# A fused transform and ELU layer: contiguous row pairs, channel-128 sums moved one step later, and a tile's first products of the fourth accumulator put off

## The chip, the cores and the metric

The kernel runs on one core of one Trainium2 chip. The metric is the device time of one execution in microseconds. The engines are named as the profile names them: PE is TensorE with PEld for its weight loads, DVE is VectorE, ACT is ScalarE, POOL is GpSimd, SP is the sync engine, which here only issues DMAs. All executions in this document are of the state "fast". A "time" is that of the whole execution; a "span" runs from the first to the last instruction on the core and is about 2 us shorter.

## The reference

```python
X = np.fft.fft(x, axis=1); X = np.fft.fft(X, axis=2)      # x: 8 x 3008 x 256, float32
h = X.real.reshape(24064, 256) @ w_in                     # w_in: 256 x 2048
g = np.where(h > 0, h, np.exp(np.minimum(h, 0)) - 1)      # ELU
out = g @ w_out                                           # w_out: 2048 x 256
```

## The kernel before

The transform over the sequence uses its symmetries: rows are folded, and cosine and sine matrices turn the folded rows into two rings, Rr and Ir. The transform over the channels is folded into w_in, which becomes Wc and Ws. Channel 128 does not fit into 128 partitions and takes a path of its own. Its values are transformed with eight partitions, summed there (`ext_rows`), and broadcast into the ring Rb and row 127 of Ir.

The body is a list of 376 steps. Each makes two blocks of 128 hidden units for 256 columns:

```python
at(t + 0.0,  mm_P)         # TensorE: H  = Wc * Rr
at(t + 0.9,  even_part)    # VectorE: E  = Rb * wex + H
at(t + 2.17, mm_Q)         # TensorE: H += Ws * Ir          (after E has read H)
at(t + 3.55, h_minus)      # VectorE: second half of the outputs
... two activations each on ScalarE and VectorE (g_plus, g_minus), one step later
WINOGRAD = (sum_1, sum_3, sum_2, sum_4 on GpSimd,           # T + 2.91 to 2T + 0.3
            (2 * T + 0.87, mm_X1), (2 * T + 3.04, mm_X2))   # TensorE, seven products
```

`T` is 4.8, a nominal step; the times only fix the order on each engine. Eight steps make a tile of output columns in four PSUM accumulators, pA to pD. When a tile is full VectorE combines them, and the next tile reuses the same banks; this is called the turn of a tile below:

```python
def mm_X2(i):
    ...
    prod(i, 2, 0, wt(i, 2), 4)        # pC
    prod(i, 2, 1, wt(i, 0), 5)
    prod(i, 3, 0, wt(i, 3), 3)        # pD: in a tile's first step it waits for comb_3
    prod(i, 3, 1, w2b(i, 1, 1), 6)

COMB = ((1.45, comb_copy), (4.2, comb_1), (4.21, comb_2),
        (T + 1.0, comb_22),           # u: the last reader of pC
        (T + 2.5, comb_3))            # v: the last reader of pD
```

The parts that the change moves:

```python
# x rows behind s = 512: partition p holds rows 512 + 4(p % 64) + 2(p // 64) + 0, 1
for half in range(2):
    nc.sync.dma_start(out=L[j][64 * half : 64 * half + 64, 4 * ND :],
                      in_=xrows(b, row + 512 + 2 * half, 4, 64, 2))
...
at(33 * T + 1.46, lambda: ext_side(0)); at(33 * T + 1.47, lambda: ext_side(1))  # ScalarE copies
at(34 * T + 0.99, lambda: ext_rows(0, vtt))     # five sums on VectorE, even half
at(34 * T + 1.46, lambda: ext_side(2)); at(34 * T + 1.47, lambda: ext_side(3))
at(35 * T + 1.35, lambda: ext_rows(1, gtt))     # four sums on GpSimd, odd half
```

Of the kernel before, what the change touches and what calls it, by code (L numbers as in the profile page):

```python
# [18 lines left out]
ND = 256  # L19
# [15 lines left out]
def _dft_consts():  # L35







    p = np.arange(128)[:, None]
    out = np.zeros((128, 4, BW), np.float64)
    for ri in range(2):
        fn = np.cos if ri == 0 else np.sin
        for kodd in range(2):
            mat = out[:, 2 * ri + kodd]
            n, h = (NO, NO // 2) if kodd else (NE, NH)

            def block(m, n):
                k = 2 * np.arange(n)[None, :] + kodd
                s = 4 * p + m if m < 4 else 512 + 4 * (p % 64) + 2 * (p // 64) + m - 4
                w = np.where(s == 0, 0.5, 1.0) * (s <= RUN)
                w = np.where(s == RUN, 0.5 if ri == kodd else 0.0, w)
                return s, w * fn(2.0 * np.pi * ((s * k) % SEQ) / SEQ)

            for m in (0, 2, 4):
                s, v = block(m, h)
                anti = (s % 4 == 2) != ri  # L60
                if not kodd:
                    v[:, h - 1] *= ~anti[:, 0]
                if m < 4:
                    c = 0 if m == 2 * ri else h
                    mat[:, c : c + h] = v
                else:
                    mat[:, 2 * h : 3 * h] = v * ~anti
                    mat[:, 3 * h : 4 * h] = v * anti
            for t in range(3):
                mat[:, BE + t * NE : BE + t * NE + n] = block(2 * t + 1, n)[1]  # L70
    return out.reshape(128, -1).astype(np.float32)
# [36 lines left out]
def kernel(  # L108
# [43 lines left out]
    def row_tables():  # L152



        for c, p0, n, base in (
            (0, 0, 128, HALF - 3),
            (1, 0, 64, HALF - 513),
            (1, 64, 64, HALF - 515),
            (2, 0, 128, HALF - 3),  # L160
            (2, 0, 1, HALF - 4),
        ):
            pin(
                nc.gpsimd.iota(
                    ix[p0 : p0 + n, c : c + 1],
                    pattern=[[0, 1]],
                    base=base,
                    channel_multiplier=-4,
                )
            )  # L170

    def load_x(b):

        L = [
            spool.tile([128, 6 * ND], FP, tag=f"xl{j}", bufs=1, name=f"xl{j}")
            for j in range(4)
        ]

        def back(j, few):
            cols = slice(0, 2 * ND) if few else slice(2 * ND, 6 * ND)  # L180
            c = 1 if few else 2 if j == 1 and b == NB - 1 else 0
            pin(
                nc.gpsimd.indirect_dma_start(  # L183
                    out=L[j][:, cols],
                    out_offset=None,
                    in_=xflat,
                    in_offset=bass.IndirectOffsetOnAxis(
                        ap=ix[:, c : c + 1].bitcast(U32), axis=0
                    ),
                    element_offset=(b * SEQ + (HALF if j == 1 else 0)) * ND,  # L190
                )
            )
            if b == NB - 1 and j == 1 and not few:
                nc.gpsimd.dma_start(
                    out=L[1][0:1, 2 * ND : 5 * ND], in_=xrows(b, SEQ - 3, 1, 1, 3)
                )

        def ahead(j, row):
            nc.sync.dma_start(out=L[j][:, 0 : 4 * ND], in_=xrows(b, row, 4, 128, 4))
            for half in range(2):  # L200
                nc.sync.dma_start(
                    out=L[j][64 * half : 64 * half + 64, 4 * ND :],
                    in_=xrows(b, row + 512 + 2 * half, 4, 64, 2),
                )

        loads = [lambda n=n: back(2 - n // 2, n % 2) for n in range(4)]
        return L, loads + [lambda: ahead(3, HALF), lambda: ahead(0, 0)]


# [472 lines left out]
    def get_ext():  # L682
        xs = state["xs"] = spool.tile([128, 4, NB, 6], FP, tag="xs", bufs=1, name="xs")
        with nc.allow_non_contiguous_dma(reason="short runs"):
            for j in range(4):
                nc.sync.dma_start(
                    out=xs[:, j, :, 0:4],
                    in_=xe_dr[j, :, 0:512].rearrange("b (p m) -> p b m", m=4),
                )
                pairs = xe_dr[j, :, 512:768].rearrange("b (p h m) -> h p b m", h=2, m=2)  # L690
                for half in range(2):
                    nc.sync.dma_start(
                        out=xs[64 * half : 64 * half + 64, j, :, 4:6], in_=pairs[half]
                    )

    def fold_ext():
        xs = state["xs"]
# [29 lines left out]
    def ext_side(g, rows=NB):  # L727
# [3 lines left out]
        act(t[0:rows, 0:n], state["ext"][32 * g : 32 * g + rows, 0:n])  # L731
        state["side", par] = t

    def ext_rows(kodd, tt, rows=NB):
        n = NO if kodd else NE
        h = (n + 1) // 2
        if not kodd or rows < NB:
            rx = spool.tile([128, HALF + 1], FP, tag="rx", bufs=1, name="rx")
            state["rx"] = rx[0:rows]
        rx, even, b = state["rx"], state["side", 0], state["side", 1][0:rows]  # L740
        a = spool.tile([128, NE], FP, tag="bs", bufs=3, name="bs")
        unfold(a, even, even[:, h : 2 * h], rows, n, tt)
        a = a[0:rows]
        o, base = 1 - kodd, kodd * RUN
        m = n - 2 * o
        tt(rx[:, base : base + n], a[:, 0:n], b[:, 0:n], ALU.add)
        top = base + RUN - 1
        tt(rx[:, top : top - m : -1], a[:, o : o + m], b[:, o : o + m], ALU.subtract)
        if not kodd:
            tt(rx[:, HALF:], a[:, 0:1], b[:, 0:1], ALU.subtract)  # L750
            nc.sync.dma_start(
                out=r4_dr.rearrange("o b -> b o"), in_=rx[:, HALF : HALF + 1]
            )
        nc.sync.dma_start(
            out=r128_dr[0:rows, base : base + RUN], in_=rx[:, base : base + RUN]
        )
# [140 lines left out]
    def wt(i, j):  # L897
        return WT[j][:, i % 8]
# [31 lines left out]
    def mm_X2(i):  # L930
        T = tiles[i // 8]
        if i % 8 == 0:
            T.acc += [bank(t) for t in ACC[2:4]]
        prod(i, 2, 0, wt(i, 2), 4)
        prod(i, 2, 1, wt(i, 0), 5)
        prod(i, 3, 0, wt(i, 3), 3)
        prod(i, 3, 1, w2b(i, 1, 1), 6)
        del steps[i]
# [300 lines left out]
    for slot in range(total):  # L1239
        i = slot % 2 * 8 + slot // 2 if slot < 16 else slot  # L1240
        t = slot * T
        begin = (
            (0.0, mm_P),
            (0.4 if slot == 0 else 0.9, even_part),
            (2.17, mm_Q),
            (3.55, h_minus),
            (4.2, below_plus),
            (4.8, below_minus),
            (T + 0.01 if slot < 16 else T + 1.5, exp_plus),
            (T + 0.02 if slot < 16 else T + 2.21, exp_minus),  # L1250
        )
        if slot == 1:
            begin = (
                (0.1 - T, mm_P),
                (0.7 - T, even_part),
                (2.6 - T, mm_Q),
                (1.5, h_minus),
                (2.95, below_plus),
                (3.0, below_minus),
                (3.01, exp_plus),  # L1260
                (3.02, exp_minus),
            )
        for dt, fn in begin + (
            (T + 2.2, g_plus),
            (T + 2.9, g_minus),
        ) + (
            (
                (2 * T + 0.87, lambda i: mm_plain(i, 0)),
                (2 * T + 3.04, lambda i: mm_plain(i, 1)),
            )  # L1270
            if i < 16
            else WINOGRAD
        ):
            at(t + dt, lambda fn=fn, i=i: fn(i))
    COMB = (
# [77 lines left out]
    at(9 * T + 4.75, dft_ext_0)  # L1353
    for g in (2, 3):
        at(10 * T + 1.46, lambda g=g: ext_side(g, 1))
    at(11 * T + 3.55, lambda: ext_rows(1, gtt, 1))
    at(11 * T + 3.6, lambda: spread_ext(0, 1))
    for n in range(16):
# [7 lines left out]
    at(32 * T + 4.75, dft_ext)  # L1366
    at(33 * T + 1.46, lambda: ext_side(0))
    at(33 * T + 1.47, lambda: ext_side(1))
    at(34 * T + 0.99, lambda: ext_rows(0, vtt))
    at(34 * T + 1.46, lambda: ext_side(2))  # L1370
    at(34 * T + 1.47, lambda: ext_side(3))
    at(35 * T + 1.35, lambda: ext_rows(1, gtt))
    fold_keys = [(k, p) for k in FOLDS for p in range(2 if k[0] not in "cx" else 1)]
    n_big = sum(k[0] not in "cx" for k, _ in fold_keys)
    for b in range(1, NB):
# [26 lines left out]
                lambda k=2 * ri + kodd: state["EO"][k],  # L1402
            )
        for kodd in range(2):
            step = s0 + (35 if late else 28, 38 + late)[kodd]
            assert step >= safe(b * HALF + (kodd + 1) * RUN)
            at(step * T + 1.0, lambda b=b, kodd=kodd: spread_ext(b, kodd))
    last = total - 40
# [49 lines left out]
```

## Time and profile before

| quantity | before |
|---|---|
| time, median of the first three runs | 1960.54 us (1960.31 to 1960.62) |
| span of the profiled run | 1958.7 us |
| PE busy | 99% of the span |
| DVE, ACT, POOL busy | 66%, 44%, 70% |
| undisturbed step | 4.75 us |
| step 34 | 9.32 us |
| granted clock in steps 34 and 35 | 0.87 and 0.90; 0.50 (the half clock below) from 227.5 to 230.9 us |

A kernel whose TensorE is busy for 99% of the span can gain only in the gaps. These are read from the waits of PE and from the lengths of the steps, each counted from one step's first Wc product to the next. A busy share hides them.

### The profile page before, as it was taken

The page shows a single profiled execution, that of the slowest core. Times are in us where ns is not written, and L with a number is a line of the kernel's source. Part 1 is how long each engine was busy: PE and PEld are TensorE (multiplying, and loading weights), DVE is VectorE, ACT ScalarE, POOL GpSimd, SP SyncE. Part 2 cuts the span into 40 slices and gives each one's busy share as a digit, 9 for nine tenths or more (in the row PEclk, how much of TensorE's full clock was granted, in tenths as well). Part 3 has the DMA queues.
Part 4 walks back from the last instruction along what each step waited for, and adds up shares of the span by engine and source line. Part 5 has one row for each costly group of instructions (what it writes and reads, how often), then busy time and mean ns, then how long its engine had stood idle before and what let it go on. Part 6 is the DMA issues. An engine that isn't in the chain of part 4 may idle for free.

```text
span 1958.7 us, 27031 instructions
## 1 busy us (share of the span) xinstructions
PE 1938.8 (99%) x8912; PEld 1652.8 (84%) x8912; DVE 1296.1 (66%) x2393; ACT 864.8 (44%) x1669; POOL 1379.6 (70%) x1821
## 2 busy tenths in 40 slices
PE   8999999999999999999999999999999999999998
PEld 5788788888888888888888888888888888888887
DVE  8976566666667666666666665676666766666666
ACT  3654344444444444444344444444434444344443
POOL 3888767776687766777677876778667776555655
PEclk9999999999999999999999999999999999999999
DMA  8246120111111021010210202002020110100101
GB/s 309 66 30 45 36 52 20 33 29 24 44 20 44 14 43 30 18 46 14 53 24 12 49 10 59 12 19 59 6 53 11 20 22 15 17 12 12 23 10 24
DMA packets 263611, 70.26 MB, mean 36 GB/s; under 512 B 248926, under 2 KB 249842, under 8 KB 263472
## 3 DMA queue, kind: packets, MB, share of 16 engines
q1 hardware_dynamic: 257680, 55.69, 15.2%
q0 software_dynamic: 3616, 12.59, 2.1%
q8 instruction: 70, 1.15, 0.2%
q14 instruction: 69, 0.57, 0.1%
q10 hardware_dynamic: 2176, 0.26, 0.1%
HBM read 43.66 MB, written 24.80 MB: 35 GB/s over the span
## 4 chain that ended last, share of the span: by engine, by line
PE 92%; POOL 2%; DVE 2%; DMA 2%; issue 1%; ACT 1%; SPq 0%; DVEq 0%; POOLq 0%; ACTq 0%
PE H L414 37%; PE pD L414 16%; PE pC L414 16%; PE pB L414 16%; PE pA L414 8%; DMA xl<-in_x_dram,ix 1%; DMA raw<-in_moe_w_out_dram 1%; POOL WT L423 1%; POOL w L423 1%; POOL G L423 0%; DMA raw<-in_moe_w_in_dram 0%; DVE E L810 0%; POOL xl L183 0%; DVE G L836 0%; DVE v L420 0%
## 5 line engine op out<-in xcount | busy, mean ns | idle before, releaser
L423 POOL TENSOR_TENSOR G<-G 128x256 f32<-128x256 f32 x1440 | 1034.6, 728 | 515.9 <-DVE G L836 343.2
L810 DVE SCALAR_TENSOR_TENSOR E<-Rb,wex,H 128x256 f32<-128x256 f32 x752 | 328.1, 478 | 582.1 <-PE H L414 578.4
L426 ACT ACTIVATE G<-H 128x512 f32<-128x512 f32 x376 | 224.5, 597 | 960.2 <-DVE G L820 960.2
L414 PE MATMUL H<-Ir,Ws 128*128 128x256 f32 x1504 | 386.9, 380 | 2.5 <-DVE E L810 1.3
L414 PE MATMUL H<-Rr,Wc 128*128 128x256 f32 x1504 | 387.7, 380 | 0.0
L414 PE MATMUL pC<-G,WT 128*128 128x256 f32 x1440 | 369.6, 379 | 1.6 <-DVE u L420 1.6
L414 PEld LDWEIGHTS H<-Rr,Wc 128*128 128x128 f32 x1504 | 285.1, 190 | 56.6 <-issue 3.4
L414 PEld LDWEIGHTS H<-Ir,Ws 128*128 128x128 f32 x1504 | 277.2, 189 | 51.9 <-DVE E L810 3.9
L414 PEld LDWEIGHTS pC<-G,WT 128*128 128x128 f32 x1440 | 273.5, 190 | 39.1 <-issue 2.0
L820 DVE SCALAR_TENSOR_TENSOR G<-E,H 128x512 f32<-128x512 f32 x376 | 257.1, 684 | 35.1 <-PE H L414 1.6
L836 DVE SCALAR_TENSOR_TENSOR G<-G,H 128x512 f32<-128x512 f32 x376 | 255.9, 681 | 21.6 <-ACT G L426 21.5
L836 DVE SCALAR_TENSOR_TENSOR G<-M,G 128x512 f32<-128x512 f32 x376 | 257.1, 684 | 0.0
L426 ACT ACTIVATE G<-G 128x512 f32<-128x512 f32 x376 | 233.2, 620 | 0.0
L414 PE MATMUL pD<-G,w 128*128 128x256 f32 x784 | 229.8, 380 | 0.7 <-POOL G L423 0.7
L414 PE MATMUL pA<-G,w 128*128 128x256 f32 x784 | 229.3, 379 | 0.6 <-DVE bs L420 0.6
L414 PE MATMUL pB<-G,w 128*128 128x256 f32 x784 | 229.3, 379 | 0.0
L426 ACT ACTIVATE M<-G 128x512 f32<-128x512 f32 x376 | 224.3, 596 | 0.0
L426 ACT ACTIVATE M<-M 128x512 f32<-128x512 f32 x376 | 221.0, 588 | 0.0
L414 PE MATMUL pD<-G,WT 128*128 128x256 f32 x720 | 215.3, 381 | 2.9 <-DVE v L420 2.5
L414 PE MATMUL pB<-G,WT 128*128 128x256 f32 x720 | 214.5, 379 | 0.2
L414 PEld LDWEIGHTS pD<-G,w 128*128 128x128 f32 x784 | 149.2, 190 | 21.4 <-POOL G L423 1.1
L414 PEld LDWEIGHTS pA<-G,w 128*128 128x128 f32 x784 | 148.9, 190 | 21.1 <-issue 0.9
(145 smaller groups left out, 1418.2 us busy)
## 6 DMA issues: line engine op xcount, KB each, us to landing
out_dram<-ot SPq DMA_DIRECT2D x496, 32.0 KB
xl<-in_x_dram SPq DMA_DIRECT2D x16, 512.0 KB
xl<-in_x_dram SPq DMA_DIRECT2D x32, 128.0 KB
out_dram<-ot SPq DMA_DIRECT2D x256, 2.0 KB
Rb<-r SPq DMA_DIRECT2D x10, 376.0 KB
raw<-in_moe_w_in_dram SPq DMA_DIRECT2D x7, 512.0 KB
MC<-dft_mats SPq DMA_DIRECT2D x3, 943.5 KB
raw<-in_moe_w_out_dram SPq DMA_DIRECT2D x4, 512.0 KB
```

Of the source, the lines that this page charges most:

```text
L414: nc.tensor.matmul(out_, lhsT=lhsT, rhs=rhs, start=start, stop=stop, skip_group_check=True)
L423: pin(nc.gpsimd.tensor_tensor(out=o, in0=a, in1=b, op=op))
L426: pin(nc.scalar.activation(out=o, in_=i, func=func, **kw))
L810: nc.vector.scalar_tensor_tensor(out=S.E[:, c], in0=Rb[:, cols(i)], scalar=wex[:, f : f + 1], in1=S.H[:, c], op0=ALU.mult, op1=ALU.add,)
L820: nc.vector.scalar_tensor_tensor(out=two(S.G[:, 0:512])[:, :, ::-1], in0=two(S.E), scalar=2.0, in1=two(S.H), op0=ALU.mult, op1=ALU.subtract,)
L836: nc.vector.scalar_tensor_tensor(out=o, in0=e, scalar=-1.0, in1=h, op0=ALU.add, op1=ALU.max)
```

## The change

Its intent has three parts. Two contiguous rows per partition behind s = 512 make one DMA of two. The channel-128 sums of the even half leave step 34, which also turns a tile over, for VectorE's gap in step 35; those of the odd half leave GpSimd in step 35 for VectorE's gap in step 36. And in a tile's first step the products into pD come after the next step's Wc products, so that they need not wait for v.

```diff
-   s = 4 * p + m if m < 4 else 512 + 4 * (p % 64) + 2 * (p // 64) + m - 4
+   s = 4 * p + m if m < 4 else 508 + 2 * p + m
    (the row tables and the loads of channel 128 follow; one iota and one DMA of each pair go)
-   for half in range(2):
-       nc.sync.dma_start(out=L[j][64 * half : 64 * half + 64, 4 * ND :],
-                         in_=xrows(b, row + 512 + 2 * half, 4, 64, 2))
+   nc.sync.dma_start(out=L[j][:, 4 * ND :], in_=xrows(b, row + 512, 2, 128, 2))
    ...
+   def ext_unfold(kodd, tt, rows=NB): ...        # the first two sums of ext_rows, cut off
    ...
+   def mm_X3(i):
        prod(i, 3, 0, wt(i, 3), 3)
        prod(i, 3, 1, w2b(i, 1, 1), 6)
    ...
+   X3 = ((3 * T + 0.1 if i % 8 == 0 else 2 * T + 3.05, mm_X3),)
    ...
-   at(34 * T + 0.99, lambda: ext_rows(0, vtt))
-   at(34 * T + 1.46, lambda: ext_side(2))
-   at(34 * T + 1.47, lambda: ext_side(3))
-   at(35 * T + 1.35, lambda: ext_rows(1, gtt))
+   at(35 * T + 0.2, lambda: ext_unfold(0, vtt))
+   at(35 * T + 1.5, lambda: ext_rows(0, vtt))
+   at(35 * T + 4.75, lambda: ext_side(2))
+   at(35 * T + 4.76, lambda: ext_side(3))
+   at(36 * T + 0.2, lambda: ext_unfold(1, vtt))
+   at(36 * T + 1.5, lambda: ext_rows(1, vtt))
    (the broadcast of the even half goes from step 35 to step 37)
```

More of the change, by code (lines that the diff above doesn't have):

```diff
@@ L152, in row_tables @@
     def row_tables():
-        for c, p0, n, base in (
-            (0, 0, 128, HALF - 3),
-            (1, 0, 64, HALF - 513),
-            (1, 64, 64, HALF - 515),
-            (2, 0, 128, HALF - 3),
-            (2, 0, 1, HALF - 4),
+        for c, n, base, step in (
+            (0, 128, HALF - 3, -4),
+            (1, 128, HALF - 513, -2),
+            (2, 128, HALF - 3, -4),
+            (2, 1, HALF - 4, 0),
         ):
@@ L164, in row_tables @@
                 nc.gpsimd.iota(
-                    ix[p0 : p0 + n, c : c + 1],
+                    ix[0:n, c : c + 1],
                     pattern=[[0, 1]],
                     base=base,
-                    channel_multiplier=-4,
+                    channel_multiplier=step,
                 )
@@ L199, in ahead @@
             nc.sync.dma_start(out=L[j][:, 0 : 4 * ND], in_=xrows(b, row, 4, 128, 4))
-            for half in range(2):
-                nc.sync.dma_start(
-                    out=L[j][64 * half : 64 * half + 64, 4 * ND :],
-                    in_=xrows(b, row + 512 + 2 * half, 4, 64, 2),
-                )
+            nc.sync.dma_start(
+                out=L[j][:, 4 * ND :], in_=xrows(b, row + 512, 2, 128, 2)
+            )
         loads = [lambda n=n: back(2 - n // 2, n % 2) for n in range(4)]
@@ L689, in get_ext @@
                 )
-                pairs = xe_dr[j, :, 512:768].rearrange("b (p h m) -> h p b m", h=2, m=2)
-                for half in range(2):
-                    nc.sync.dma_start(
-                        out=xs[64 * half : 64 * half + 64, j, :, 4:6], in_=pairs[half]
-                    )
+                nc.sync.dma_start(
+                    out=xs[:, j, :, 4:6],
+                    in_=xe_dr[j, :, 512:768].rearrange("b (p m) -> p b m", m=2),
+                )
     def fold_ext():
@@ L732, in ext_side, with ext_unfold @@
         state["side", par] = t
+    def ext_unfold(kodd, tt, rows=NB):
+        n = NO if kodd else NE
+        h = (n + 1) // 2
+        even = state["side", 0]
+        a = spool.tile([128, NE], FP, tag="bs", bufs=3, name="bs")
+        unfold(a, even, even[:, h : 2 * h], rows, n, tt)
+        state["es"] = a[0:rows]
     def ext_rows(kodd, tt, rows=NB):
         n = NO if kodd else NE
-        h = (n + 1) // 2
         if not kodd or rows < NB:
@@ L739, in ext_rows @@
             state["rx"] = rx[0:rows]
-        rx, even, b = state["rx"], state["side", 0], state["side", 1][0:rows]
-        a = spool.tile([128, NE], FP, tag="bs", bufs=3, name="bs")
-        unfold(a, even, even[:, h : 2 * h], rows, n, tt)
-        a = a[0:rows]
+        rx, a, b = state["rx"], state["es"], state["side", 1][0:rows]
         o, base = 1 - kodd, kodd * RUN
@@ L1271 @@
             if i < 16
-            else WINOGRAD
+            else WINOGRAD + X3
         ):
@@ L1355 @@
         at(10 * T + 1.46, lambda g=g: ext_side(g, 1))
+    at(11 * T + 3.54, lambda: ext_unfold(1, gtt, 1))
     at(11 * T + 3.55, lambda: ext_rows(1, gtt, 1))
@@ L1404 @@
         for kodd in range(2):
-            step = s0 + (35 if late else 28, 38 + late)[kodd]
+            step = s0 + (37 if late else 28, 38 + late)[kodd]
             assert step >= safe(b * HALF + (kodd + 1) * RUN)
```

## The prediction

> **What bounds the kernel now.** I read the page first, then TensorE's own waits, then a table of stretches cut at the starts of the steps, then the order of instructions inside the stretches that stood out. The page gives TensorE 1938.8 of 1958.7 us, and its chain of the work that ended last is 92% TensorE.
>
> ```profile
> PE 1938.8 (99%) x8912; PEld 1652.8 (84%) x8912; DVE 1296.1 (66%) x2393; ACT 864.8 (44%) x1669; POOL 1379.6 (70%) x1821
> ...
> PE 92%; POOL 2%; DVE 2%; DMA 2%; issue 1%; ACT 1%; SPq 0%; DVEq 0%; POOLq 0%; ACTq 0%
> ```
>
> The change removes no matmul: as many products, transforms and transposes run as before. An undisturbed step starts 22 TensorE records and takes 4.75 us (241.57 to 246.32). The change can win only where TensorE stands still or runs at a lower clock. Its waits, longest first (total us, times, longest):
>
> ```profile
> PE pC L414 <- DVE xe L420: 3.1, 1, 3.1
> PE pD L414 <- DVE v L420: 2.5, 4, 1.0
> PE pC L414 <- DVE u L420: 1.6, 1, 1.6
> PE H L414 <- DVE E L810: 1.3, 3, 0.6
> ```
>
> The first falls at 15 us in the start-up. The second and third are the change's aim: pC and pD are the third and fourth accumulator, whose first product of a new tile waits until VectorE has combined the old tile (u reads pC, v reads pD). The table of stretches, one step each (columns: length, busy time of PE, PEld, DVE, ACT, POOL, then granted clock, DMA):
>
> ```profile
> 220.58:229.90 9.32, 6.42 (x24) 4.46 (x23) 7.59 (x15) 3.91 (x8) 5.15 (x8) 0.87 0.16 40
> 229.90:235.16 5.26, 5.26 (x23) 4.54 (x22) 3.38 (x6) 2.10 (x5) 5.10 (x8) 0.90 0.03 7
> 235.16:241.57 6.41, 6.29 (x29) 5.12 (x28) 3.38 (x6) 2.47 (x5) 6.10 (x9) 1.00 0.33 51
> 241.57:246.32 4.75, 4.75 (x23) 4.15 (x22) 3.19 (x7) 1.79 (x4) 2.70 (x5) 1.00 0.54 104
> ```
>
> Step 34 takes 9.32 instead of 4.75 us, steps 35 and 36 lose some more, and the clock is down in the first two. Step 36 holds half a transform beside its products (1.28 us by its matmuls), so only 6.41 - 4.75 - 1.28 = 0.4 of it is waiting. Inside step 34:
>
> ```profile
> 223.09 1.30 DVE L420 TENSOR_TENSOR bs<-side 8x189 f32<-8x189 f32 x2
> ...
> 224.43 1.07 DVE L420 TENSOR_TENSOR rx<-bs,side 8x377 f32<-8x377 f32 x3
> ...
> 225.43 0.40 DVE L420 TENSOR_TENSOR u<-v,pC 128x256 f32<-128x256 f32 x1
> ...
> 225.59 0.48 ACT L426 ACTIVATE side<-H 8x376 f32<-8x376 f32 x1 [0.63 <-DVE rx L420]
> ...
> 225.97 1.10 PE L414 MATMUL pC<-G,WT 128*128 128x256 f32 x4 [1.61 <-DVE u L420]
> ...
> 227.23 0.68 DVE L420 TENSOR_TENSOR v<-v,pD 128x512 f32<-128x512 f32 x1
> ...
> 228.06 1.19 PE L414 MATMUL pD<-G,WT 128*128 128x256 f32 x2 [0.98 <-DVE v L420]
> ```
>
> Five channel-128 sums (2.34 us of VectorE) stand ahead of u, in the one step that also has to turn a tile over. They hold u, u holds pC; ScalarE waits for them with its next copies and passes the delay to the activation, to v and to pD.
>
> [...] The lower clock costs 9.32 x 0.13 + 5.26 x 0.10 = 1.7 us. [...] the first bs took 1039 ns beside a GpSimd fold that ended at 223.92, the second, of the same size and alone, 335. [...] this run shows only the cost of issuing, 1.19 us for two of them.
>
> **The change part by part.**
>
> Row pairs. Each batch's load issues two DMAs fewer on the sync engine, of about 0.6 us each, and the start-up one row-table instruction of 0.13 us fewer on GpSimd. Bytes and packet sizes stay (2 KB rows). In the first 16 us the DMA engines run at 300 to 400 GB/s nearly throughout, so an earlier issue only lengthens the backlog, and VectorE's first fold waits for the landing at 10.74 us. I put 0 on it, and 0.7 either way.
>
> Fourth accumulator. A list of the tile turns shows v late for pD at eight of them: step 34 and seven others. Counting start to start against the usual 216 ns and the slow refill behind each wait, four of the seven (472, 517, 913 and 1441 us) lose 0.32 us and three (956, 1001, 1398 us) lose 0.78, 0.71 and 0.78: 3.55 us. The rest lose nothing; there v ends 0.42 us before pD starts. Put off behind the next step's first four records, these products start 0.86 us later, more than the wait. But what then comes sooner has limits of its own. At 956 us the step's next product group would reach its third pair, which needs GpSimd's third sum, at 955.93 + 3 x 0.86 = 958.52, and that sum ends at 957.17 + 2 x 0.75 = 958.67 or so: with the refill, about 0.35 us of the 0.78 comes back. At the short turns the sum is in time (474.1 against 474.4). So 4 x 0.32 + 3 x 0.42 = 2.5 us.
>
> Channel-128 sums. I walk step 34 to 36 by the measured spacings (0.61 us for an activation pass on VectorE, 0.78 for the pair of E, 0.86 for four TensorE records). Step 34: u at 223.09, in time for pC at 224.2; the activation pass, v, and the other passes run through to 225.9. TensorE begins step 35 at 225.06. Step 35 on VectorE: unfold 225.9 to 227.1 (two operations of 0.34 alone, a GpSimd sum in the way of each), E to 228.0, in time for TensorE, which wants it by 228.08; three sums to about 229.3; two passes, h and a transpose to 231.8. VectorE is full by then. Step 36 begins on TensorE at 230.67. ScalarE copies the odd half only after step 35's h, at 231.75 to 232.7, so the second unfold starts at 232.25 and ends[...] between 233.3 and 233.9; E(36) ends near 234.4. TensorE wants it at 232.83. So I expect one new wait of 1.4 to 2.0 us before the Ws products of step 36. Then 234.45 + 3 x 0.86 + 1.28 + 0.1 of refill: step 37 at 238.4 instead of 241.57, a gain of 3.1 us, v's late pD of step 34 and the old clock loss in it. A new wait of 1.6 us in one piece may bring the half clock back. [...] I give it 4 in 10, so 0.4 x 1.7 = 0.7 off: 2.4 us.
>
> Moving the odd sums from GpSimd frees it of 3.0 us in step 35 and with it the 0.4 us of waiting for GpSimd's sums in step 36; that is in the walk. The broadcast of the new row to Rb now goes out after the stores of tile 3, near 242 us; it is first read in step 40, near 254, so it is hidden.
>
> Sum: 2.4 + 2.5 + 0 = 4.9, and 1960.5 - 4.9 = 1955.6; I take 1955.4, since the walk places contention on every operation.
>
> **Rivals.** (a) The new wait at step 36 does not occur, because VectorE finds GpSimd idle at the right moments or ScalarE copies sooner. For it: before the change VectorE stood idle 2.38 and 1.22 us ahead of E in steps 35 and 36, which is what the change wants to fill. Against it: with 2.3 us more in each of two steps that have 2.6 us of passes and a 0.6 us transpose, VectorE needs about 5.5 of the 5.6 us that step 35 then lasts[...]. It would make 1952.7. (b) VectorE becomes the bound for the two steps and the half clock returns: gain near step 34 about 1 us, and 1957.5. (c) The products put off collide with what follows, so that the seven turns move their wait on to GpSimd's sums or to a bank of H: then only the four short ones gain, 1.3 us, and the whole gives 1956.7. (d) Start-up: earlier issued matrices delay the x rows that VectorE waits for; 0.5 to 1 us worse.
>
> **Range and chances.** Everything in play is TensorE waiting of 5.5 us around steps 34 to 36 and 3.55 us at seven turns; all of it together would give 1951.4 without start-up effects. (a) bounds the likely side below at about 1952, (b) with (d) above at about 1958.3. A change of 2% is 39 us, four times all of it, so the answer is "within 2%" almost surely.
>
> **What would show it.** Right, if step 34 shrinks to about 4.5 us with no wait for u; if no turn shows TensorE waiting for v; if the odd unfold runs on VectorE in step 36 beside a wait of TensorE for E of over a microsecond; and if the three long turns show a short wait for GpSimd's sums. Wrong, if steps 35 to 36 show no wait (then faster than I say), if a second half-clock window of 3.4 us stands near 235 us (slower), if the first product on TensorE starts more than 0.7 us off its 28.54, or if a turn that lost nothing before waits now.

## The result and the profile after

The changed kernel took 1953.19 us in the median (1952.0 to 1954.94, four runs) against 1960.58 (1960.31 to 1960.75, four runs). The ratio is 0.9963, 95% interval 0.9946 to 0.998. A ratio here is the mean time of one kernel's fast runs over that of the other's of the same rounds, so it is not quite the ratio of the medians quoted. By the 2% rule this is "same". The profiled run was the slowest of the four.

From the page of the changed kernel, busy times and the shares of the chain that ended last:

```profile
PE 1936.6 (99%) x8912; PEld 1653.8 (85%) x8912; DVE 1299.7 (67%) x2397; ACT 865.1 (44%) x1669; POOL 1378.4 (71%) x1816
...
PE 93%; DVE 3%; POOL 2%; issue 1%; DMA 1%; ACT 1%; SPq 0%; DVEq 0%; POOLq 0%
```

As many matmuls as before, and still 99%: the page alone would not say that anything happened. The four extra DVE instructions and four of the five fewer on POOL are the odd sums that changed engine. PE's own waits (total us, times, longest) do say it:

```profile
PE pC L410 <- DVE xe L416: 3.2, 1, 3.2
PE H L410 <- DVE E L809: 2.6, 4, 1.2
...
PE pD L410 <- POOL G L419: 0.7, 1, 0.7
```

The waits of pD for v (2.5 us) and of pC for u (1.6 us) are gone. The waits for E rose from 1.3 to 2.6 us in all, 1.2 of it in one piece. The steps 34 to 37 of the changed kernel (length, then busy times, clock, DMA share, GB/s):

```profile
220.90:225.38 4.48, 4.17 (x20) 3.23 (x19) 4.38 (x9) 2.12 (x4) 3.92 (x6) 1.00 0.00 0
225.38:230.99 5.61, 5.61 (x28) 4.87 (x27) 5.61 (x11) 2.12 (x4) 3.47 (x5) 1.00 0.02 4
230.99:238.84 7.85, 6.56 (x30) 5.04 (x29) 6.63 (x13) 4.26 (x8) 5.93 (x9) 1.00 0.24 38
238.84:243.59 4.75, 4.75 (x24) 4.16 (x23) 3.19 (x7) 1.81 (x4) 3.11 (x5) 1.00 0.39 70
```

Step 34 is only 4.48 us long because its pD products (0.86 us) now run in step 35, which is that much longer; 0.59 us of it is still a wait for E with its refill (the product behind the first one started 0.32 us after it, where 0.22 is usual; the step takes 3.89 us in odd38_side below). The clock stays at 1.00. Steps 34 to 36 together take 17.94 us instead of 20.99: 3.05 us less. In step 35 DVE (third busy figure) works for all 5.61 us. The price is in step 36: 7.85 us, of which 4.75 are a step's own work and 1.28 half a transform. The order of instructions shows where the rest goes:

```profile
223.41 0.41 DVE L416 TENSOR_TENSOR u<-v,pC 128x256 f32<-128x256 f32 x1
...
224.51 1.03 PE L410 MATMUL pC<-G,WT 128*128 128x256 f32 x4
...
226.13 1.31 DVE L416 TENSOR_TENSOR bs<-side 8x189 f32<-8x189 f32 x2
...
228.15 1.77 DVE L416 TENSOR_TENSOR rx<-bs,side 8x377 f32<-8x377 f32 x3
...
232.38 0.98 ACT L422 ACTIVATE side<-H 8x376 f32<-8x376 f32 x2
...
232.88 1.14 DVE L416 TENSOR_TENSOR bs<-side 8x188 f32<-8x188 f32 x2 [0.55 <-ACT side L422]
...
233.95 0.85 DVE L809 SCALAR_TENSOR_TENSOR E<-Rb,wex,H 128x256 f32<-128x256 f32 x2
...
234.86 1.13 PE L410 MATMUL H<-Ir,Ws 128*128 128x256 f32 x4 [1.22 <-DVE E L809]
```

The number in brackets is the engine's idle time before the instruction. In step 34, u is done well before pC asks for it. In step 36 the odd sums wait for ScalarE's copy, E waits for the odd sums, and PE waits 1.22 us for E.

At the seven other tile turns no wait for v is left. The three long ones keep a shorter one of another kind; the turn at 952 us of the changed kernel:

```profile
953.45 2.34 POOL L419 TENSOR_TENSOR G<-G 128x256 f32<-128x256 f32 x3 [0.40 <-DVE G L835]
...
955.04 0.70 PE L410 MATMUL pB<-G,WT 128*128 128x256 f32 x2
```

The pB products would have started at 954.81 after the pair before them. They need the second of the three sums in the POOL line, and the step loses 0.34 us where it lost 0.78.

### The profile page after: what moved, and what is told of

It is laid out like the page before. It is cut to its first block, busy times and chain, and to the rows that moved or that the text cites. A ratio compares the mean times of both kernels' runs of the same rounds, so it can differ in the third digit from the quotient of the medians.

```text
span 1953.2 us, 26991 instructions
## 1 busy us (share of the span) xinstructions
PE 1936.6 (99%) x8912; PEld 1653.8 (85%) x8912; DVE 1299.7 (67%) x2397; ACT 865.1 (44%) x1669; POOL 1378.4 (71%) x1816
## 4 chain that ended last, share of the span: by engine, by line
PE 93%; DVE 3%; POOL 2%; issue 1%; DMA 1%; ACT 1%; SPq 0%; DVEq 0%; POOLq 0%
PE H L410 37%; PE pC L410 16%; PE pD L410 16%; PE pB L410 16%; PE pA L410 8%; POOL WT L419 1%; POOL w L419 1%; POOL G L419 0%; DMA xl<-in_x_dram 0%; DVE E L809 0%; DVE e L504 0%; DVE G L835 0%; DVE o L504 0%; DVE pow L310 0%; DMA xl<-in_x_dram,ix 0%
```

## The experiments

Eleven runs were made, nine of new kernels and two repeats, all with correct results. Differences of one or two microseconds are not safe in the medians, because the start-up turned out to move by that much (see below). So I read every kernel twice: by its time, and by its steps in one profile. "Start" is the first Wc product of step 0, "0 to 37" the time from there to that of step 37, "37 to 372" the time from there to that of step 372. One difference in the column "0 to 37" belongs to no edit: step 4 took 6.91 to 6.93 us in eight profiles, with one wait of PE for GpSimd's weight work of 0.6 us, and 6.36 or 6.37 us without it in five (same_again, dft_late, halves_back, sel_dft, sel_dft_x).

| kernel | median us | ratio to before | start | 0 to 37 | 37 to 372 |
|---|---|---|---|---|---|
| before | 1960.58 | | 28.54 | 213.03 | 1685.01 |
| changed | 1953.19 | 0.9963 | 28.86 | 209.98 | 1682.47 |
| rows_only | 1960.54 | 0.9994 | 28.71 | 213.14 | 1684.89 |
| x3_only | 1959.35 | 0.9994 | 28.86 | 213.07 | 1682.66 |
| ext_only | 1959.09 | 0.9991 | 29.47 | 209.97 | 1684.91 |
| whole_again | 1953.88 | 0.9966 | 26.42 | 210.00 | 1682.27 |
| same_again | 1961.81 | 1.0003 | 29.61 | 212.51 | 1685.07 |
| x_first | 1953.81 | 0.9965 | 25.86 | 210.06 | 1682.52 |
| odd38_side | 1951.58 | 0.9952 | 28.32 | 207.90 | 1682.49 |
| dft_late | 1956.12 | 0.9974 | 28.56 | 209.47 | 1684.51 |
| halves_back | 1955.41 | 0.9975 | 30.20 | 209.40 | 1682.42 |
| sel_dft | 1950.05 | 0.9949 | 26.82 | 207.28 | 1681.61 |
| sel_dft_x | 1948.16 | 0.9939 | 26.19 | 207.29 | 1681.21 |

**rows_only.** The kernel before with the first part of the diff alone.

```diff
+   s = ... 508 + 2 * p + m       # with its row tables, loads and channel-128 loads, nothing else
```

> The kernel before with the row pairs alone (new order of rows behind 512, one DMA in place of two, one row-table instruction fewer). Theory A (the start-up is free of it on average, as predicted): 0 against before, within 0.7 us, and as steady as before (spread under 0.5 us). Theory B (the 2.2 us by which the whole change beat my number come from here, and so does the spread of 1952.0 to 1954.9 that the kernel before does not have): 1 to 3 us faster in the median, with single runs spread over 1.5 us or more, and the first product of step 0 between 25.5 and 29 us instead of 28.54, moved by the landing of the first x rows.

The runs fell into two groups: 1958.15 and 1958.70, and 1960.54 to 1961.08. The spans do the same: twice 1956.3, and 1958.2, 1958.4, 1958.6, while the nine runs of the kernel before beside them had 1958.2 to 1959.2. So theory B holds in part: the spans are spread, two of five are some 2.3 us shorter, and in their mean the edit is worth 1958.68 - 1957.56 = 1.1 us, with five runs. Its gain of 1 to 3 us in the median did not come (1960.54 against 1960.63), and the profiled run is one of the longer ones. The DMA view of the first 16 us tests the reason for my zero. The kernel before:

```profile
DMA packets 1638, 4.40 MB, mean 275 GB/s; under 512 B 201, under 2 KB 329, under 8 KB 1638
```

and rows_only:

```profile
DMA packets 1907, 5.17 MB, mean 323 GB/s; under 512 B 205, under 2 KB 333, under 8 KB 1907
```

The DMA engines had room: between 5.6 and 7.2 us the kernel before moved only 169 to 225 GB/s, where rows_only moved 302 to 343. With two issues fewer, the sync engine gets the next loads out earlier: in the changed kernel the transform matrices at 3.79 us against 5.61, the second weight chunk at 6.10 against 7.80. And 18% more has arrived by 16 us. So an earlier issue did more than lengthen the backlog. That it brings the x rows sooner is not shown here: in this profile VectorE's first fold began at 10.91 us against 10.74.

The same run answers a question that I had not asked. Its steps 34 to 36:

```profile
220.82:229.24 8.42, 5.52 (x24) 3.82 (x23) 7.49 (x15) 3.15 (x6) 4.33 (x7) 1.00 0.06 17
229.24:233.99 4.75, 4.75 (x24) 4.16 (x23) 3.49 (x7) 2.88 (x6) 4.51 (x7) 1.00 0.19 58
233.99:241.85 7.86, 6.29 (x30) 5.12 (x28) 3.38 (x6) 2.46 (x5) 7.55 (x11) 1.00 0.27 42
```

It has the same two gaps for u and v, and no half clock: 1.00 in all three steps. Steps 34 and 35 are 1.4 us shorter than before the change. Yet the three together are 21.03 us against 20.99, because step 36 waits. From PE's waits in this stretch of rows_only:

```profile
PE pB L411 <- POOL G L420: 1.6, 1, 1.6
```

GpSimd, which has the odd sums in step 35 in this version, is late with its sums for step 36. At half clock PE simply arrived later and waited less: in the kernel before no wait for GpSimd is listed between 200 and 245 us. So the 1.7 us that I charged to the lower clock cost nothing on balance in this order of work; GpSimd's odd sums were the bound right behind it.

**x3_only.** The kernel before with `mm_X3` alone.

```diff
+   X3 = ((3 * T + 0.1 if i % 8 == 0 else 2 * T + 3.05, mm_X3),)
```

> The kernel before with the fourth accumulator's first products put off, nothing else. By my walk: 2.5 us less at the seven turns, no wait for v at them, a wait of 0.25 to 0.35 us for GpSimd's third sum at the three long turns; step 34 still waits for u (1.6 us) and the half clock stays, so at most 0.9 us there, perhaps given back to GpSimd's sums: 1957.2 to 1958.2, as steady as before. Rival (put-off products collide with an H bank or with the sums at every turn): under 1.3 us.

Steps 37 to 372 took 1682.66 us against 1685.01: 2.35 us less, where I had worked out 2.5. From 0 to 37 there was no gain at all, and the waits in that stretch name the reason:

```profile
PE pB L414 <- POOL G L423: 2.1, 2, 2.0
```

The pD products no longer waited, but in step 36 those into pB waited for GpSimd instead. The half clock, which I had expected to stay, did not come (mean clock 0.999 in the profiled run, 0.997 in that of the kernel before), and it made no difference. The time expected was missed (1959.35, not 1957.2 to 1958.2, and its runs are spread over 2.3 us). The start of 28.86 us in the profile explains only 0.3 us of that; same_again below takes it up.

**ext_only.** The kernel before with the sums in steps 35 and 36 alone.

```diff
-   at(34 * T + 0.99, lambda: ext_rows(0, vtt))  ...  at(35 * T + 1.35, lambda: ext_rows(1, gtt))
+   at(35 * T + 0.2, ext_unfold(0)) ... at(36 * T + 1.5, ext_rows(1))       # both on VectorE
```

> The kernel before with the channel-128 sums in steps 35 and 36, nothing else. By my walk: no wait for u or v in step 34, one wait of 1.2 to 1.6 us for E in step 36, no half clock: 3.1 us less, 1957.2 to 1957.8, as steady as before. Rival (moving the even sums only shifts the wait): under 1.5 us less.

From 0 to 37: 209.97 against 213.03, 3.06 us less, as worked out; from 37 on nothing. The median again misses (1959.09); its profiled run began step 0 at 29.47 us. By the steps the parts add up: 2.35 + 3.06 = 5.4, and the changed kernel has 3.05 + 2.54 = 5.6 in one profile and 3.03 + 2.74 = 5.8 in the other.

**whole_again.** The changed kernel once more.

```diff
    (none against the changed kernel)
```

> The changed kernel once more. It shows how far apart its runs lie (1952.0 to 1954.9 so far) beside the kernel before on the same chip, and gives a second profile, whose start-up can be laid beside the first. Theory A: the spread has nothing to do with the row pairs, and the three parts run alone are spread too. Theory B: the start of step 0 moves from run to run with the landing of the x rows, and all later steps keep their lengths to within 0.3 us in all; if step 0 began at 28.86 us in a run of 1954.9, it begins near 26 us in a run of 1952.

1953.88 us (1952.16 to 1955.35). Its steps agree with the first profile within 0.2 us; its start does not, 26.42 against 28.86 us. The first fold on VectorE waits for the x rows from the middle on. In the changed kernel's first profile (start us, length, and in brackets the idle time before):

```profile
11.07 0.96 DVE L504 TENSOR_TENSOR e<-xl 128x768 f32<-128x768 f32 x1 [4.65 <-DMA xl<-in_x_dram]
```

and in the second:

```profile
8.62 0.96 DVE L504 TENSOR_TENSOR e<-xl 128x768 f32<-128x768 f32 x1 [2.20 <-DMA xl<-in_x_dram]
```

Same program, same queue order, 2.45 us apart; step 0 moves by 2.45. In all 13 profiles step 0 began 17.79 to 17.81 us after this fold, so the fold sets the start. Theory B holds. Theory A keeps one point: x3_only and ext_only, which have no row pairs, were spread too, by 2.3 and 1.5 us.

**same_again.** The kernel before, submitted as a change.

```diff
    (none against the kernel before)
```

> The kernel before, submitted as if it were a change: a control for the start-up. The three part kernels began step 0 at 28.7 to 29.5 us, two of them with the start-up code of the kernel before, which began at 28.54. Theory A (the start moves by chance from run to run and from loading to loading): runs spread over 1 us or more around 1960, first product of step 0 anywhere from 27.5 to 29.5. Theory B (it belongs to the program): 1960.2 to 1961.5 as in the twelve runs so far, step 0 at 28.5 within 0.2.

1961.81 us (1960.61 to 1962.81), start 29.61 us. Its nine companions gave 1959.77 to 1962.26. So theory A holds for the kernel before: its start, too, moves by about a microsecond from run to run, and from 28.54 it went only later. That accounts for a part of why x3_only and ext_only look slower by the clock than by their steps. In the mean of the spans they gained 1.4 and 2.0 us, about 1.0 less each than by the steps, and same_again came out 0.35 us longer than its companions. So the mean start of five runs can lie up to a microsecond off with nothing changed in the start-up; what decides it stays open.

**x_first.** The changed kernel with the two loads of the x rows from the middle on put first in the sync engine's queue.

```diff
+   L_first, loads = load_x(0)
+   loads[4]()
    w1_chunks[0].load()
    nc.sync.dma_start(out=CC, in_=CC_dr.ap())
-   L_first, loads = load_x(0)
-   for load in loads:
+   for load in loads[:4] + loads[5:]:
        load()
```

> The changed kernel with the load of the x rows from the middle on moved to the front of the sync engine's queue, ahead of the first weights. If the landing of these rows is what step 0 waits for, the first fold on VectorE begins at 8 us or before in every run (8.6 in one profile of the changed kernel, 11.1 in the other), and the time is 1951 to 1952.5 with the spread under 1 us. If the start hangs on something else, such as the reversed rows or the first weights, no better than 1953.5 and as spread as before.

1953.81 us, spans 1950.4 to 1952.9: no better and as spread as the changed kernel. In its profile the fold began at 8.07 us, but the run profiled was one of the fast ones. The x rows no longer held it: their recorded completions had all come by 4.85 us, and VectorE had waited for the first weights, until 6.66 us. The expectation of a steady start failed: the place in the queue does not decide it alone, and what held the slow runs, which have no profile, is not known.

**odd38_side.** The odd sums two steps later, and the even copies behind step 33's activation.

```diff
-   at(33 * T + 1.46, lambda: ext_side(0))       # and 1.47, ext_side(1)
+   at(33 * T + 4.75, lambda: ext_side(0))       # and 4.76
-   at(36 * T + 0.2, lambda: ext_unfold(1, vtt)) # and 1.5, ext_rows
+   at(38 * T + 0.2, lambda: ext_unfold(1, vtt)) # and 1.5
```

> The changed kernel with the odd channel-128 sums two steps later (step 38, which has no tile turn and no transform to unfold), and with ScalarE's copies of the even half put behind the activation of step 33, as the change did with the odd half. By my reading the wait for E in step 36 (1.4 us with the refill, and 0.33 for GpSimd's sum ahead of it) goes, and the wait for E in step 34 (0.57): 2.2 to 2.4 us less from step 33 to step 39 than in the changed kernel. If VectorE is full there whatever the order, less than 1 us.

From 0 to 37 it took 207.90 us against 209.98: 2.1 us less, nearly all of the 2.2 to 2.4. Both waits for E (steps 34 and 36) are gone from PE's waits between 200 and 260 us, which are an empty list. In step 36 (6.30 us) some 0.27 us of waiting for GpSimd's sum is left. The median is 1951.58. No work was taken from VectorE; another order was enough.

**dft_late.** Each transform's VectorE work behind the two activation passes.

```diff
-   at(t + T + 1.01, lambda: d().plus())         # and 1.02, minus; 1.0, unfold
+   at(t + T + 2.95, lambda: d().plus())         # and 2.96, 2.95, from step 28 on
```

> The changed kernel with each transform's VectorE work placed behind the two activation passes instead of ahead of them, from step 28 on. If the three long turns wait for GpSimd's third sum because the transform's work holds back the activation pass that GpSimd starts from (my prediction's step), their 0.35, 0.28 and 0.35 us go and nothing else changes: 0.9 to 1.0 us less over the steps. Rival (the wait comes from GpSimd's own fold piece or its row gathers): they stay. Risk: VectorE's next passes come later and a new wait appears.

A miss that teaches something: 1956.12 us. The waits for GpSimd at the three long turns are gone, as my reading of them requires. But eight new waits for E came; from PE's waits after 240 us, those long enough to be listed:

```profile
PE H L410 <- DVE E L809: 1.1, 3, 0.4
```

Counted by steps against the changed kernel, the eight lose 0.26 us (five) and 0.58 to 0.59 (three, which lost 0.07 to 0.14 there already); 37 to 372 grew by 2.0 us. In a step just before a turn's products the late work pushes h and the combining of the tile, and with them the next E.

**halves_back.** The changed kernel's rows, loaded again in two halves.

```diff
-   nc.sync.dma_start(out=L[j][:, 4 * ND :], in_=xrows(b, row + 512, 2, 128, 2))
+   for half in range(2):
+       nc.sync.dma_start(out=L[j][64 * half : 64 * half + 64, 4 * ND :],
+                         in_=xrows(b, row + 512 + 128 * half, 2, 64, 2))
```

> The changed kernel with its two contiguous row pairs per partition kept, but each of these loads issued again as two DMAs over 64 partitions. It parts the layout from the number of DMAs. If the second issue sets the start (in the kernel before the second half landed at 10.6 us or later in every profile[...]), then no run is among the fast ones: spans of 1952.5 us or more, against 1950.2 to 1953.2 in nine runs of the changed kernel, median 1955 or so. If the contiguous layout alone does it, or chance, the spans spread from 1950 to 1953 as in the changed kernel.

1955.41 us, spans 1951.8 to 1954.4, mean 1953.2 against 1951.6 of whole_again: 1.6 us worse. Two runs lay below the bound that I had set (1952.4 and 1951.8 against 1952.5), so its spans overlap those of the changed kernel. The fold began at 12.41 us in its profile:

```profile
12.41 0.96 DVE L506 TENSOR_TENSOR e<-xl 128x768 f32<-128x768 f32 x1 [6.32 <-DMA xl<-in_x_dram]
```

In the kernel before, which also has two DMAs but not the contiguous layout:

```profile
10.74 0.96 DVE L508 TENSOR_TENSOR e<-xl 128x768 f32<-128x768 f32 x1 [4.25 <-DMA xl<-in_x_dram]
```

So the number of DMAs, and not the contiguous layout, is the likelier cause. All profiles agree: with two DMAs for these rows the fold began at 10.74 us or later in five of five; with one, in its old place in the queue, at 8.62 and 9.03 us in two and at 10.52 to 11.07 in four. Over all runs, taking as the start a run's span less the time from step 0 to the end in its kernel's profile (good to the half microsecond of step 4), 11 of 28 with one DMA in that place started before 27.0 us, and none of 47 with two before 27.5. A single DMA allowed an early start here; it did not ensure it. The two kernels compared here ran in different calls, each with a kernel before beside it (means of spans 1958.68 and 1958.28), which makes the difference rather larger than smaller.

**sel_dft.** odd38_side, and the transform's work put behind the activation passes only where it shares a step with a tile's combining.

```diff
+   late = 1.94 if step >= 28 and step % 8 == 1 else 0
-   at(t + T + 1.01, lambda: d().plus())
+   at(t + T + 1.01 + late, lambda: d().plus())          # minus and unfold alike
```

> The version with the odd sums in step 38 and the even copies later, and in addition the transform's VectorE work placed behind the two activation passes, but only in the steps that turn a tile over. Everywhere (the run before) it cured the three long turns and made new waits of 0.27 to 0.72 us for E one step later; those stood in turn steps whose preceding step held a transform. So here the 0.35, 0.29 and 0.35 us go and no new wait comes: 0.9 to 1.0 us less than that version from step 0 to step 372 (1890.4 by its profile, so about 1889.4), median near 1950.6. If the work only moves its wait, no gain.

37 to 372: 1681.61 against 1682.49, 0.9 us less; the three waits are gone and no new one came. The median is 1950.05. The 0.6 us from 0 to 37 are not its doing: they lie in step 4, where the two kernels have the same order.

**sel_dft_x.** The same with the x rows first in the queue.

```diff
+   loads[4]()                                           # as in x_first
```

> The same with the x rows first in the sync engine's queue. That order alone gave no better median than the changed kernel and the same spread, so I expect 0 to 0.4 us against the version without it; if one late engine decides the start, the two groups of runs, some 2.4 us apart, stay.

1948.16 us (1948.06 to 1949.33), ratio 0.9939 with interval 0.9925 to 0.9953, and steady: spans 1946.1 to 1946.7. That is better than the 0 to 0.4 us that I expected. The two groups did not stay, so in this kernel the queue order did help, where it did not in x_first. In its profile the fold began at 8.40 us, straight behind the work on the first weights, and step 0 at 26.19. Why it was steady here and not in x_first I cannot say. It is the fastest version here, ahead of the kernel before and of the changed one. One wait of PE is left after 240 us, for GpSimd beside its row gathers:

```profile
PE pD L410 <- POOL G L419: 0.4, 1, 0.4
```

## Why the prediction was right or wrong

The time lay in the range, 2.2 us below the number: 1953.19 against 1955.4. Point by point:

- **Fourth accumulator, 2.5 us.** Right. It measured 2.35 us alone and 2.5 to 2.7 in the whole. The part given back at the three long turns, put at 0.35 each, measured 0.34, 0.28 and 0.35, and dft_late and sel_dft showed that its cause is the one named: the activation pass that GpSimd's sums start from.
- **Channel-128 sums, 3.1 us from the walk.** Right: 3.05. The walk had step 35 begin on TensorE at 225.06, the second unfold start at 232.25 and the new wait be 1.4 to 2.0 us; in the profile, which runs 0.3 us late from the start, it is 225.38, 232.88, and 1.22 us of idle time or 1.4 from start to start (1.60 us between two products, where 0.22 is usual). One item was missed, 0.33 us for GpSimd's third sum ahead of it; it cost nothing, because E, which does not depend on it, came later still, and PE only waited that much less for E.
- **"4 in 10, so 0.4 x 1.7 = 0.7 off".** The half clock did not return: the clock was 1.00 in steps 34 to 37 of the changed kernel's first profile, and the mean clock of both its profiled runs was 0.999. The 4 in 10 was an estimate of mine; how much idle time brings the half clock was not shown (last section). Its price was mis-sized too, for the old order: in rows_only the same gaps brought no half clock and steps 34 to 36 were no shorter. What it would have cost in the new order no run shows.
- **Row pairs, "I put 0 on it".** This is the step that failed; its 1.5 us or so and the 0.7 us above make up the difference. The reason I gave, that "an earlier issue only lengthens the backlog", was wrong: the view of the first 16 us has 275 GB/s in the mean and 169 to 225 at its lowest after the rise. The fold does wait for the landing of these rows, as I had it, but only with a single DMA did it start as early as 8.6 us. What stands in place of the 0 is 1.1 us less in the mean alone (five runs), and 1.6 us more when the second DMA is put back. Which time within 1952.0 to 1954.9 came out was chance: the start moves from run to run.
- **Rivals.** (a), no new wait, did not happen; that the result is close to its 1952.7 is luck, through the start. (b) did not happen. (c) was right around step 34 of x3_only; of the seven turns only the three long ones moved a part of their wait, as the estimate had it. (d) is the opposite of what happened. The times of (a) and (b) are 0.5 us off the prediction's own terms: 3.1 + 1.6 + 2.5 less gives 1953.3, and 1 + 2.5 less gives 1957.0.
- **Signs named in advance.** Four that would show it right came true. Of those against it one came true, in the second profile: the first product of step 0 lay at 26.42 us, 2.1 from 28.54.

The parts sum to 5.6 us by the steps. The means of all spans differ by more: 1958.68 against 1951.52 over nine runs of the changed kernel, 7.2 us. The remaining 1.6 us are the start, and rows_only and halves_back agree in sign and size; with a spread of 3 us in nine runs, and kernels with an unchanged start-up that came out up to a microsecond later, it cannot be fixed better.

What stays open: why the load of the x rows lands 2.4 us later in some runs of one program, and why putting it first in the queue steadied the start in one kernel and not in the other. Of the completion records of that DMA one or two came late: in the first profile eight of nine had come by 9.03 us and one came at 10.97; in the second all ten had come by 8.52. In rows_only, odd38_side and dft_late, too, the last one or two came at 10.28 to 10.81 us and the rest by 9.41. That a late DMA engine is behind it, as I supposed before sel_dft_x, was not shown. No experiment touched it.

## What to carry to other kernels

When one engine is busy for 99% of the time, cut the run into its steps and compare their lengths with the undisturbed one; nearly every excess of 0.3 us or more had a name in the waits, and a walk with measured durations through three steps was good to 0.1 us here. Work that only has to be done some time belongs in a step without other extra work on that engine: two steps later it was free, in the first gap that looked wide enough it cost 1.4 us. Before a lower clock or a wait is charged, look at which wait stands behind it, and compare small changes by steps as well as by total times, since the start may move by more than they are worth (by 2.45 us here).

## What else the profiles show

- The half clock. In the kernel before the clock was 0.50 from 227.5 to 230.9 us. In the 3.40 us ahead of that (224.1 to 227.5) PE had a product running for only 1.36 us, the rest being the wait for u (1.61 us) and the first 0.43 us of the wait for v (0.98 us). In the changed kernel the stretch from 231.46 to 234.87 us, with 1.29 us of idle time, was followed by a clock of 1.00. same_again has the same two gaps as the kernel before and a clock of 0.88 in step 34; rows_only has them, too, and 1.00. So the two gaps alone do not decide it, and what does was not shown.
- At this start-up the second DMA for the same rows cost 1.6 us of 1953 in the mean span of five runs each (halves_back 1953.2, whole_again 1951.6).
- VectorE beside GpSimd: the same three sums took 1.07 us in the kernel before, with GpSimd idle, and 1.77 us in the changed kernel, beside a fold.
- Two profiles of one program differ by 2.45 us in the start of the work that waits for one 256 KB load behind a 512 KB one, and by as much in the start of step 0.
